# Two chains of attention layers: all seven product banks in one rotation, and a new table of ten value phases

## The chip, the cores and the metric

The kernel runs on one core of a Trainium2 chip. Five engines matter here: TensorE (PE in the profile; its weight loads are the row PEld), VectorE (DVE), ScalarE (ACT), GpSimd (POOL) and the queue of SyncE (SP) that issues the DMAs. The metric is the time of one execution on the device in microseconds; before the change it is 5680.44 us, the median of three runs (5678.14 to 5684.44).

## The reference, cut to what matters

Four residual layers run in the order A, B, A, B over one sequence of 2048 tokens with 576 features. In both kinds there are 32 heads of 18 features; in B all heads share one key and one value.

```python
S, D, H, Dh = 2048, 576, 32, 18
def _A_ref(x, wqkv, wo):
    q, k, v = (x @ wqkv) split into 3, H heads of Dh
    scores = einsum("bhqd,bhkd->bhqk", q, k) * (Dh ** -0.5)
    p = softmax(scores)
    return einsum("bhqk,bhkd->bhqd", p, v) @ wo        # heads joined again
def _B_ref(x, wq, wk, wv, wo):                          # the same, k and v without a head
...
x = x + _A_ref(_layernorm(x), A_wqkv, A_wo)
x = x + _B_ref(_layernorm(x), B_wq, B_wk, B_wv, B_wo)
x = x + _A_ref(_layernorm(x), A_wqkv, A_wo)
x = x + _B_ref(_layernorm(x), B_wq, B_wk, B_wv, B_wo)
```

Nearly all the work is the attention: per layer 32 heads of 2048 by 2048 scores, their exponentials, and the product with the values.

## The kernel before, in words

**Layers and units.** Each layer projects queries, keys and values (`project`, `natural`), attends, and projects the result back (`out_proj`). The attention goes by pairs of heads (`p`, 16 of them) and by quarters of 512 queries (`u`): 64 units a layer, 256 in all. A unit needs three kinds of product on TensorE:

- *scores* (`exp_mm`, L789 to L799): keys on the partitions, 512 queries along the free axis, 32 of them a unit (16 blocks of 128 keys for each head of the pair). The matmul is L795; ScalarE turns each bank into exponentials (L799, `pt<-pse`).
- *maxima* (`max_mm`, L556 to L589): the row maxima that the exponent subtracts have to be known first, so they come from a separate product with queries on the partitions and 512 keys along the free axis (L576), 32 a unit. VectorE reduces each bank to one column (L581, `mx<-psm`). Four times a unit two such products are *shared*: the product with the difference of two key blocks (L570) goes to ScalarE as a ReLU into the one SBUF tile `relu` (L574), and the product with the first of the two blocks is later joined with it on VectorE (L579, a custom instruction that adds and takes the maximum). So of 32 maximum products a unit ScalarE takes 4 and VectorE 28. `m_order` (L530 to L542) pairs each shared product with a partner: the first product of the same head that lies more than three products later and is not taken.
- *values* (`pv_block`, L812 to L829): exponentials times values into one bank, `oacc`, with 19 columns a head (18 features and a one that yields the sum). The 512 columns of one step of four exponentials can be cut anywhere, and `pv_cols` (L803) asks for so many columns at a time. After 8 steps, or 4096 columns, a unit is complete and ScalarE copies `oacc` out (L827, `oc<-oacc`).

The two heads of a pair lie on partitions 0 to 63 and 64 to 127, and a score or maximum product uses only its head's half of the array; two neighbouring products of different heads run side by side. Score and maximum products (512 columns wide) and value products use the array in different ways, so the kernel groups them.

**The order of the work.** It is written out by hand in `UNIT` (L65), a list of phases. Each phase is a row of products, such as `m0 e1 e0 m1 e0 m1` (`m` maximum, `e` score, the digit is the head), and a number of value columns to be done after it. Eleven phases make a unit: 32 scores, 32 maxima, 4096 columns. The maxima run ahead of the scores by `LEAD` = 14 steps of four, so those of a unit are complete shortly after the third phase of the unit before; `UNIT_X` (L73) lists which of the unit's 32 maxima are shared ones. The loop that walks the table is L925 to L936; the first two phases of a layer do no value columns. When the last maximum is done, a shorter loop (L940) finishes the scores.

**The banks.** One of the eight PSUM banks is `oacc`. Maxima take turns in three banks (`mtile`, L144) and scores in four (`etile`, L147). A product can't start before the reader of the bank's last product is done: for a score always ScalarE, for a maximum VectorE (ScalarE for a shared one). The projections outside the loop and the maxima that are woven into them use the same two functions.

**Small steps in the loop.** Once a unit `max_final` (L769) takes 128x32 to 128x8 on VectorE (L771, `neg<-mx`), GpSimd splits it, `max_store` (L777) transposes it on VectorE (L780, `tr<-hl`), and SyncE sends it through DRAM into two rows of the query tile (L782, L786). `o_sum`, `l_part`, `l_inv`, `l_out`, `l_rows`, `o_mul` and `o_out` normalise a finished unit on GpSimd with some DMAs. They stand in `todo` with due times counted in scores, and `run_todo` issues at the start of a phase what has come due.

Of the kernel before, what the change touches and what calls it, by code (L numbers as in the profile page):

```python
# [8 lines left out]
F32 = mybir.dt.float32  # L9
# [9 lines left out]
P = 128  # L19
NCH = S // P  # L20
NPAIR = H // 2
# [25 lines left out]
LEAD = 14  # L47
# [14 lines left out]

UNIT = [("m0 e1 e0 m1 e0 m1", 512), ("m0 e1 m1 e0 e1 m0", 416), ("e0 m1 m0 e1 e0 e1 m0", 416),  # L65
        ("m0 m1 e1 e0 m1", 192), ("e1 m0 m1 e0 e1 m0", 544), ("m1 e0 e0 m1 m0 e1", 352), ("e0 m1 e1 m0 m0 e1", 416),
        ("e0 m1 e0 e1 m1 m0 e1", 384), ("m0 m1", 32), ("e1 m0 e0 e1 e0 m1 m0", 448), ("e1 m0 m1 e0 e0 m1", 384)]
UNIT = [([(o[0], int(o[1])) for o in rows.split()], cols) for rows, cols in UNIT]

UNIT_X = (9, 17, 24, 30)  # L73


@with_exitstack
def tile_kernel(ctx: ExitStack, tc: tile.TileContext, A_x, A_wqkv, A_wo, B_x, B_wq, B_wk, B_wv, B_wo, out):
# [6 lines left out]
    psum = ctx.enter_context(tc.tile_pool(name="psum", bufs=1, space=PSUM))  # L84
# [56 lines left out]
        nc.gpsimd.memset(t, 0.0)  # L141


    def mtile(name):  # L144
        return psum.tile([P, 512], F32, tag="m", bufs=3, name=name)

    def etile(name):  # L147
        return psum.tile([P, 512], F32, tag="e", bufs=4, name=name)

    def ptile(name, shape=(P, 512), dt=F32):  # L150
        return pool.tile(list(shape), dt, tag="p", bufs=15, name=name)
# [208 lines left out]
    tail = []  # L360
# [31 lines left out]
    for layer in range(4):  # L392
# [125 lines left out]
        def ops(p):  # L518
            return big[:, q_slot(p)], big[:, k_slot(p)]


        m_next, m_done, m_count, m_full = [0, 0], [0], {}, []
# [6 lines left out]

        m_order, m_diff = [], set()  # L530
        for a in range(2):
            cycle = [g for rows, _ in UNIT for kind, g in rows if kind == "m"]
            n = -4 * LEAD % 32
            own = [(i, i % 32 in UNIT_X) for i in range(n, n + 32) if cycle[i % 32] == a]
            order = [None] * 16
            for qc, i in enumerate(i for i, x in enumerate(own) if x[1]):
                order[i] = qc, 1
                order[min(j for j, (at_, x) in enumerate(own) if at_ > own[i][0] + 3 and not x and not order[j])] = qc, 0
                m_diff.add((a, qc, 1))
            left = [(i // 2 % 4, i // 8 * 2 + i % 2) for i in range(16)]  # L540
            left = [x for x in left if x not in order]
            m_order.append([x or left.pop(0) for x in order])  # L542

        def max_place(a, i):

            p, u = divmod(i // 16, 4)
            if i < len(m_first):
                return (0, *m_first[i])
            n = i % 16
            return (p, u, *m_order[a][n]) if i >= 32 else (p, u, n // 2 % 4, n // 8 % 2 * 2 + n % 2)  # L550


        ns = STEPS * 4 * NPAIR
        m_heads = ([0, 1] * (2 * LEAD) + [g for rows, _ in UNIT for kind, g in rows if kind == "m"] * (4 * NPAIR))[:4 * ns]

        def max_mm(bank=mtile):  # L556

            i = m_done[0]
            a = m_heads[i]
            p, u, qc, kb = max_place(a, m_next[a])  # L560
            q, k = ops(p)
            if (p, u) not in mxs:
                mxs[p, u] = pool.tile([P, 32], F32, name="mx") if (p, u) < (0, 2) else mx2[u % 2]
            mx, ps = mxs[p, u], bank("psm")
            b, r = 64 * a, 16 * a + 4 * qc + kb
            c0 = u * 512 + qc * P
            if (p, u) >= (0, 2) and (a, qc, kb) in m_diff:
                assert kd_pair[p % 2 if is_a and p else 2] == (p if is_a else 0)
                k = kd(p)[b:b + 3 * DH]
                nc.tensor.matmul(ps.rearrange("p (h t) -> p h t", h=2) if p == 0 or not is_a else ps,  # L570
                                 q[b:b + 3 * DH, c0:c0 + P], k,
                                 start=True, stop=True)
                t = relus[p, u, a, qc] = relu[:, :512]
                nc.scalar.activation(t, ps, AF.Relu)  # L574
            else:
                nc.tensor.matmul(ps, q[b:b + KM, c0:c0 + P], k[b:b + KM, kb * 512:(kb + 1) * 512], start=True, stop=True)  # L576
                if kb == 0 and (p, u, a, qc) in relus:
                    t = relus.pop((p, u, a, qc))
                    nc.vector.tensor_tensor_reduce(t, ps, t, 1.0, LOWEST, OP.add, OP.max, mx[:, r:r + 1])  # L579
                else:  # L580
                    nc.vector.reduce_max(mx[:, r:r + 1], ps, axis=AX.X)  # L581
            m_next[a] += 1
            m_done[0] += 1
            while m_full and i >= m_full[0][1] + 2:
                max_final(*m_full.pop()[0])
            m_count[p, u] = m_count.get((p, u), 0) + 1
            if m_count[p, u] == 32:
                assert m_next[0] == m_next[1]
                m_full.append(((p, u), i))  # L589
# [3 lines left out]
        def kd(p):  # L593
            if p == 0 or not is_a:
                return big[:, 1::4, 7 * 256:]
            i = p % 2
            return xx_flat[:, 512 * i:512 * i + 512]
# [171 lines left out]
        def max_final(p, u):  # L769
            neg = pool.tile([P, 8], F32, name="neg")  # L770
            nc.vector.tensor_reduce(neg, mxs.pop((p, u)).rearrange("p (b k) -> p b k", k=4), axis=AX.X, op=OP.max,  # L771
                                    negate=True)
            hl = nms[p, u] = hls[(4 * p + u) % 2]
            copy(nc.gpsimd, hl[:, 0:8], neg)
            nc.gpsimd.tensor_tensor(hl[:, 8:16], neg, hl.bitcast(F32)[:, 0:8], op=OP.subtract)
# [10 lines left out]
                nc.sync.dma_start(big_f[64 * a + KM:64 * a + KE, q_slot(p), u * 512:(u + 1) * 512],  # L786
                                  m_d[u][:, a].rearrange("j q p -> j (q p)"))

        def exp_mm(p, u, i, tail):  # L789

            a, kc = (i // 2) % 2, i // 4 * 2 + i % 2
            q, k = ops(p)
            e = (mtile if tail and i % 2 else etile)("pse")
            r = 64 * a
            nc.tensor.matmul(e, k[r:r + KE, kc * P:(kc + 1) * P], q[r:r + KE, u * 512:(u + 1) * 512],  # L795
                             start=True, stop=True)

            pt = pts[p, u, i] = ptile("pt")
            nc.scalar.activation(pt, e, AF.Exp, scale=SCALE)  # L799
# [3 lines left out]
        def pv_cols(cols):  # L803

            while cols:
                n, c0 = divmod(pv_at[0], 512)
                w = min(cols, 512 - c0)
                pv_block(n, c0, c0 + w)
                pv_at[0] += w
                cols -= w  # L810

        def pv_block(n, c0, c1):  # L812

            p, u, i = *divmod(n // STEPS, 4), n % STEPS * 4
            cs = slice(c0, c1)
            turn[0] += 1
            for i in range(i, i + 4) if turn[0] % 2 else range(i + 3, i - 1, -1):
                a, kc = (i // 2) % 2, i // 4 * 2 + i % 2
                j = 64 * a + 32 * (kc % 2)
                nc.tensor.matmul(oacc[j:j + DH + 1, cs], v_of(kc)[:, 2 * p + a if is_a else 0, :], pts[p, u, i][:, cs],  # L820
                                 start=kc < 2 and c0 == 0, stop=kc >= 14 and c1 == 512)
                if c1 == 512:
                    pts.pop((p, u, i))
            if c1 == 512 and i // 4 == STEPS - 1:
                oc = ocs[p, u] = ptile("oc")
                if m_done[0] < 4 * ns:
                    nc.scalar.activation(oc, oacc, AF.Copy)  # L827
                else:
                    copy(nc.vector, oc, oacc)  # L829
# [43 lines left out]
        for p in range(NPAIR):  # L873
            for u in range(4):
                b = STEPS * (4 * p + u) + STEPS - 1
# [14 lines left out]
        for c in range(5):  # L890
# [3 lines left out]
            if layer < 3:  # L894
                b = LEAD + 32 * (NPAIR - 1) + 2 * c
# [6 lines left out]
        def run_todo(st):  # L902
            for n in sorted(n for n in todo if n <= st):
                for f, args in todo.pop(n):
                    f(*args)

        b = LEAD + ns
# [9 lines left out]
        assert not weave["left"] and m_done[0] == 4 * LEAD  # L917
        e_next = [0, 0]

        def exp_next(a):  # L920
            pu, kc = divmod(e_next[a], NCH)
            exp_mm(*divmod(pu, 4), kc // 2 * 4 + 2 * a + kc % 2, m_done[0] >= 4 * ns)
            e_next[a] += 1

        phase = 0  # L925
        while m_done[0] < 4 * ns:
            rows, cols = UNIT[phase % len(UNIT)]
            run_todo(LEAD + sum(e_next) / 4)
            for kind, a in rows:
                if kind == "e":  # L930
                    exp_next(a)
                elif m_done[0] < 4 * ns:
                    max_mm()
            if phase >= 2:
                pv_cols(cols)
            phase += 1  # L936
        while m_full:
            max_final(*m_full.pop()[0])
# [12 lines left out]
        tail = [todo.pop(n, []) for n in range(ns + LEAD + L_AT + 1, ns + LEAD + O_AT)]  # L951
# [32 lines left out]
```

## Time and profile before

| | |
|---|---|
| median of 3 runs | 5680.44 us (5678.14 to 5684.44) |
| profiled execution, span | 5684.0 us (3.6 us above the median; the profile gives no other time for it) |
| PE busy | 5650.3 us, 99% |
| PEld busy | 3010.8 us, 53% |
| DVE busy | 4917.2 us, 87% |
| ACT busy | 4932.6 us, 87% |
| POOL busy | 1836.8 us, 32% |
| from the start of one unit's scores to the next, inside the loop | 18.9 us |

The span has four stages that look alike, one a layer: some 200 us of projections, in which VectorE and ScalarE are partly idle, then close to 1200 us of the loop. A busy time is the time in which at least one instruction of the engine was running; instructions of one engine overlap in the records, so a busy share near 100% doesn't say that nothing more would fit in. In the rows of the timeline the columns are the start, the length, the engine, the line and operation, and how many instructions of that kind the row joins; brackets tell for how long the engine was idle before it and which work released it.

### The profile page before, as it was taken

To read this page: it belongs to the slowest core of one execution; us is meant where nothing else is said; L and a number is where in the kernel's file an instruction comes from. 1 tells how busy PE (TensorE), PEld (TensorE's weight loads), DVE (VectorE), ACT (ScalarE), POOL (GpSimd) and SP (SyncE) were. 2 spreads that over 40 slices of the span, in tenths; PEclk is the share of its full clock that TensorE was granted. 3 is DMA by queue.
4 is the path that set the end of the run, shared out by engine and by line. 5 is a ranking of instruction groups with operands and counts; after the bars stand their busy time and mean duration, and the time that the engine had idled before them with its cause. 6 is when DMAs were issued, how large, how long until landed. Compare 5 with 4: busy or idle time off the path is not lost.

```text
span 5684.0 us, 148130 instructions
## 1 busy us (share of the span) xinstructions
PE 5650.3 (99%) x57758; PEld 3010.8 (53%) x57758; DVE 4917.2 (87%) x9489; ACT 4932.6 (87%) x9872; POOL 1836.8 (32%) x2396
## 2 busy tenths in 40 slices
PE   9999999999999999999999999999999999999999
PEld 8644444444844444444686444444448444444446
DVE  4799999997699999999637999999976999999995
ACT  2599999999289999999726999999992999999996
POOL 3243333334233333233312433333332332323232
PEclk9999999999999999999999999999999999999999
DMA  6321111111420000001253211111114100000002
GB/s 206 120 58 42 44 44 45 42 44 26 128 68 23 23 21 23 20 23 24 60 172 105 54 47 41 46 42 46 39 34 130 56 23 23 23 24 20 23 15 79
DMA packets 275207, 301.97 MB, mean 53 GB/s; under 512 B 135247, under 2 KB 193191, under 8 KB 265215
## 3 DMA queue, kind: packets, MB, share of 16 engines
q1 hardware_dynamic: 274502, 292.49, 18.4%
q8 instruction: 453, 7.42, 0.5%
q14 instruction: 252, 2.06, 0.1%
HBM read 168.50 MB, written 119.86 MB: 51 GB/s over the span
## 4 chain that ended last, share of the span: by engine, by line
PE 95%; POOL 1%; DMA 1%; issue 1%; DVE 1%; SPq 0%; ACT 0%; POOLq 0%; DVEq 0%; ACTq 0%
PE oacc L820 37%; PE pse L795 23%; PE psm L576 18%; PE psn L240 6%; PE psm L570 5%; PE psq L414 5%; DVE mx L581 1%; PE ps L232 0%; POOL big L186 0%; DMA raw<-in_B_wk_dram 0%; DMA m_d<-tr 0%; DMA big<-qk_d 0%; DMA big<-m_d 0%; DMA qk_d<-ev 0%; POOL ev L426 0%
## 5 line engine op out<-in xcount | busy, mean ns | idle before, releaser
L799 ACT ACTIVATE pt<-pse 128x512 f32<-128x512 f32 x8192 | 4262.6, 642 | 98.8 <-PE pse L795 61.8
L581 DVE TENSOR_REDUCE mx<-psm 128x1 f32<-128x512 f32 x6208 | 3931.1, 685 | 313.0 <-PE psm L576 132.7
L576 PE MATMUL psm<-big 62*128 62x512 f32 x7200 | 2665.8, 452 | 7.1 <-DMA big<-qk_d 4.0
L795 PE MATMUL pse<-big 64*128 64x512 f32 x8192 | 2411.4, 429 | 5.6 <-ACT pt L799 3.3
L820 PE MATMUL oacc<-pt,vbuf 128*19 128x96 f32 (+3 forms) x27536 | 1754.9, 361 | 3.5 <-DVE oc L157 3.5
L795 PEld LDWEIGHTS pse<-big 64*128 64x128 f32 x8192 | 1191.8, 185 | 784.5 <-ACT pt L799 602.3
L576 PEld LDWEIGHTS psm<-big 62*128 62x128 f32 x7200 | 1164.1, 184 | 381.4 <-DVE mx L581 231.6
L820 PEld LDWEIGHTS oacc<-pt,vbuf 128*19 128x19 f32 x27536 | 530.2, 98 | 782.2 <-issue 652.0
L157 POOL TENSOR_SCALAR os<-oc 32x512 f32<-32x512 f32 x512 | 314.5, 614 | 1923.1 <-ACT oc L827 1532.3
L846 POOL TENSOR_TENSOR rl<-lt,mone 128x8 f32<-128x8 f32 x256 | 423.2, 1653 | 1099.4 <-DMA lt<-os 1045.4
L579 DVE CUSTOM_DVE_ANT_0 relu<-psm,relu 128x512 f32<-128x512 f32 x992 | 676.7, 682 | 0.0
L574 ACT ACTIVATE relu<-psm 128x512 f32<-128x512 f32 x992 | 616.2, 621 | 1.5 <-PE psm L570 0.8
L820 PE MATMUL oacc<-pt,vy 128*19 128x256 f32 (+3 forms) x9168 | 591.4, 360 | 0.0
L422 ACT ACTIVATE ev<-psq 128x512 fp32r<-128x512 f32 (+1 forms) x112 | 67.1, 599 | 335.0 <-PE psq L414 233.3
L820 PEld LDWEIGHTS oacc<-pt,vy 128*19 128x19 f32 x9168 | 206.0, 98 | 267.9 <-issue 220.0
L859 POOL TENSOR_TENSOR os<-os,rb 96x512 f32<-96x512 f32 x256 | 327.8, 1280 | 27.4 <-DMA rb<-r_d 26.3
L837 POOL TENSOR_TENSOR os<-os,oc 96x512 f32<-96x512 f32 x256 | 327.0, 1277 | 21.4
L240 PE MATMUL psn<-wsm,xx 128*128 128x288 f32 x2240 | 308.0, 296 | 0.0
L240 PEld LDWEIGHTS psn<-wsm,xx 128*128 128x128 f32 x2240 | 298.7, 188 | 12.9 <-issue 11.6
L428 DVE TENSOR_TENSOR ev<-psq,ev 128x512 fp32r<-128x512 f32 (+1 forms) x84 | 58.0, 691 | 213.5 <-ACT ev L422 199.6
L570 PE MATMUL psm<-big 54*128 54x512 f32 x512 | 240.7, 470 | 0.0
L570 PE MATMUL psm<-xx,big 54*128 54x512 f32 x480 | 225.0, 469 | 0.0
(93 smaller groups left out, 2378.8 us busy)
## 6 DMA issues: line engine op xcount, KB each, us to landing
big<-qk_d SPq DMA_DIRECT2D x172, 432.0 KB
qk_d<-ev SPq DMA_DIRECT2D x96, 512.0 KB
qk_d<-ev SPq DMA_DIRECT2D x120, 256.0 KB
rb<-r_d SPq DMA_DIRECT2D x512, 36.0 KB
o_d<-os SPq DMA_DIRECT2D x512, 36.0 KB
m_d<-tr SPq DMA_DIRECT2D x1024, 2.0 KB
o<-o_d SPq DMA_DIRECT2D x64, 256.0 KB
xx<-qk_d SPq DMA_DIRECT2D x120, 72.0 KB
```

Of the source, the lines that this page charges most:

```text
L240: nc.tensor.matmul(ps, lhs[:, xc, :], wsm[:, wc, h * 288:(h + 1) * 288], start=i == 0, stop=i == len(TERMS) - 1)
L570: nc.tensor.matmul(ps.rearrange("p (h t) -> p h t", h=2) if p == 0 or not is_a else ps, q[b:b + 3 * DH, c0:c0 + P], k, start=True, stop=True)
L574: nc.scalar.activation(t, ps, AF.Relu)
L576: nc.tensor.matmul(ps, q[b:b + KM, c0:c0 + P], k[b:b + KM, kb * 512:(kb + 1) * 512], start=True, stop=True)
L579: nc.vector.tensor_tensor_reduce(t, ps, t, 1.0, LOWEST, OP.add, OP.max, mx[:, r:r + 1])
L581: nc.vector.reduce_max(mx[:, r:r + 1], ps, axis=AX.X)
L795: nc.tensor.matmul(e, k[r:r + KE, kc * P:(kc + 1) * P], q[r:r + KE, u * 512:(u + 1) * 512], start=True, stop=True)
L799: nc.scalar.activation(pt, e, AF.Exp, scale=SCALE)
L820: nc.tensor.matmul(oacc[j:j + DH + 1, cs], v_of(kc)[:, 2 * p + a if is_a else 0, :], pts[p, u, i][:, cs], start=kc < 2 and c0 == 0, stop=k ...
L837: nc.gpsimd.tensor_tensor(t[:96], t[:96], oc[:96], op=OP.add)
L846: nc.gpsimd.tensor_tensor(rl, lts.pop((p, u)), mone, op=OP.pow)
L859: nc.gpsimd.tensor_tensor(t[:96], t[:96], rb[:96], op=OP.mult)
```

## The change

All seven banks go into one list ordered by last use. In the loop a product no longer takes the next bank of its own kind: it takes the bank longest unused (rank 0) or the second longest unused (rank 1), whoever reads it, and the third character in the table gives the rank. Outside the loop `mtile` and `etile` still take turns over three and four banks. The table has ten phases instead of eleven, all with six or seven products, and the kind `r` marks a shared maximum in the table itself: three a unit in place of four, all of head 1, at the places 14, 16 and 26 among the unit's 32 maxima (counted from 0). `m_order` gives them the partners 18, 21 and 31. The 928 value columns that the first two phases of a layer skipped are now counted out by `PV_LAG`; the first two phases of the new table have 928 columns as well.

```diff
-UNIT = [("m0 e1 e0 m1 e0 m1", 512), ("m0 e1 m1 e0 e1 m0", 416), ("e0 m1 m0 e1 e0 e1 m0", 416),
-        ("m0 m1 e1 e0 m1", 192), ("e1 m0 m1 e0 e1 m0", 544), ("m1 e0 e0 m1 m0 e1", 352), ("e0 m1 e1 m0 m0 e1", 416),
-        ("e0 m1 e0 e1 m1 m0 e1", 384), ("m0 m1", 32), ("e1 m0 e0 e1 e0 m1 m0", 448), ("e1 m0 m1 e0 e0 m1", 384)]
-UNIT = [([(o[0], int(o[1])) for o in rows.split()], cols) for rows, cols in UNIT]
-UNIT_X = (9, 17, 24, 30)
+UNIT = [("e01 m10 e00 m10 m00 e11", 384),
+        ("m10 e00 m10 e00 e10 m01", 544),
+        ("e10 m01 e10 m01 m10 e00", 384),
+        ("e10 m00 e10 e00 m10 e01", 352),
+        ("m10 m00 e10 m00 e01 r10", 416),
+        ("m00 e10 r11 e00 m11 e00 m10", 416),
+        ("m01 e10 e10 e11 m00 e01 m10", 384),
+        ("m10 e00 m00 e11 m00 e11", 384),
+        ("m00 r10 e00 m01 e10 m01 e10", 416),
+        ("m11 e00 e00 m00 e10 e00 m10", 416)]
+UNIT = [([(o[0], int(o[1]), int(o[2])) for o in rows.split()], cols) for rows, cols in UNIT]
+PV_LAG = 928
+UNIT_M = [(kind, a) for rows, _ in UNIT for kind, a, _ in rows if kind != "e"]
...
+    lru, turns = list(range(7)), {"m": 0, "e": 0}
+    def bank(i, name):
+        lru.remove(i)
+        lru.append(i)
+        return psum.tile([P, 512], F32, tag=f"b{i}", bufs=1, name=name)
     def mtile(name):
-        return psum.tile([P, 512], F32, tag="m", bufs=3, name=name)
+        turns["m"] += 1
+        return bank((turns["m"] - 1) % 3, name)
     def etile(name):
-        return psum.tile([P, 512], F32, tag="e", bufs=4, name=name)
+        turns["e"] += 1
+        return bank(3 + (turns["e"] - 1) % 4, name)
+    def oldest(rank=0):
+        return lambda name: bank(lru[rank], name)
...
-            own = [(i, i % 32 in UNIT_X) for i in range(n, n + 32) if cycle[i % 32] == a]
+            own = [(i, UNIT_M[i % 32][0] == "r") for i in range(n, n + 32) if UNIT_M[i % 32][1] == a]
...
-        def exp_mm(p, u, i, tail):
+        def exp_mm(p, u, i, rank):
-            e = (mtile if tail and i % 2 else etile)("pse")
+            e = oldest(rank)("pse")
...
             rows, cols = UNIT[phase % len(UNIT)]
             run_todo(LEAD + sum(e_next) / 4)
-            for kind, a in rows:
+            for kind, a, rank in rows:
                 if kind == "e":
-                    exp_next(a)
+                    exp_next(a, rank)
                 elif m_done[0] < 4 * ns:
-                    max_mm()
-            if phase >= 2:
-                pv_cols(cols)
+                    max_mm(oldest(rank))
+            skip = min(cols, PV_LAG - lagged)
+            lagged += skip
+            pv_cols(cols - skip)
             phase += 1
```

More of the change, by code (lines that the diff above doesn't have):

```diff
@@ L60 @@
 TAIL = 2
-UNIT = [("m0 e1 e0 m1 e0 m1", 512), ("m0 e1 m1 e0 e1 m0", 416), ("e0 m1 m0 e1 e0 e1 m0", 416),
-        ("m0 m1 e1 e0 m1", 192), ("e1 m0 m1 e0 e1 m0", 544), ("m1 e0 e0 m1 m0 e1", 352), ("e0 m1 e1 m0 m0 e1", 416),
-        ("e0 m1 e0 e1 m1 m0 e1", 384), ("m0 m1", 32), ("e1 m0 e0 e1 e0 m1 m0", 448), ("e1 m0 m1 e0 e0 m1", 384)]
-UNIT = [([(o[0], int(o[1])) for o in rows.split()], cols) for rows, cols in UNIT]
-UNIT_X = (9, 17, 24, 30)
+UNIT = [("e01 m10 e00 m10 m00 e11", 384),
[11 more added lines that the diff above has]
+UNIT_M = [(kind, a) for rows, _ in UNIT for kind, a, _ in rows if kind != "e"]
+assert len(UNIT_M) == 32 and sum(cols for _, cols in UNIT) == 4096
 @with_exitstack
@@ L531, in tile_kernel @@
         for a in range(2):
-            cycle = [g for rows, _ in UNIT for kind, g in rows if kind == "m"]
             n = -4 * LEAD % 32
-            own = [(i, i % 32 in UNIT_X) for i in range(n, n + 32) if cycle[i % 32] == a]
+            own = [(i, UNIT_M[i % 32][0] == "r") for i in range(n, n + 32) if UNIT_M[i % 32][1] == a]
             order = [None] * 16
@@ L553, in tile_kernel @@
         ns = STEPS * 4 * NPAIR
-        m_heads = ([0, 1] * (2 * LEAD) + [g for rows, _ in UNIT for kind, g in rows if kind == "m"] * (4 * NPAIR))[:4 * ns]
+        m_heads = ([0, 1] * (2 * LEAD) + [a for _, a in UNIT_M] * (4 * NPAIR))[:4 * ns]
         def max_mm(bank=mtile):
@@ L918, in tile_kernel, with exp_next @@
         e_next = [0, 0]
-        def exp_next(a):
+        def exp_next(a, rank=0):
             pu, kc = divmod(e_next[a], NCH)
-            exp_mm(*divmod(pu, 4), kc // 2 * 4 + 2 * a + kc % 2, m_done[0] >= 4 * ns)
+            exp_mm(*divmod(pu, 4), kc // 2 * 4 + 2 * a + kc % 2, rank)
             e_next[a] += 1
-        phase = 0
+        phase = lagged = 0
         while m_done[0] < 4 * ns:
```

## The prediction, made before the changed kernel was run

> **What bounds the kernel now.** I read the page first, for the engines and the costliest groups:
>
> ```profile
> PE 5650.3 (99%) x57758; PEld 3010.8 (53%) x57758; DVE 4917.2 (87%) x9489; ACT 4932.6 (87%) x9872; POOL 1836.8 (32%) x2396
> ...
> L799 ACT ACTIVATE pt<-pse 128x512 f32<-128x512 f32 x8192 | 4262.6, 642 | 98.8 <-PE pse L795 61.8
> L581 DVE TENSOR_REDUCE mx<-psm 128x1 f32<-128x512 f32 x6208 | 3931.1, 685 | 313.0 <-PE psm L576 132.7
> ```
>
> Then the stage that fills most of the time, the loop of the first layer, by its busy times and by the waits of TensorE's weight loads:
>
> ```profile
> 420.00:1180.00 760.00, 760.00 (x8379) 364.16 (x8375) 714.08 (x1369) 746.51 (x1490) 264.95 (x331) 1.00 0.17 44
> ```
>
> ```profile
> PEld pse L795 <- ACT pt L799: 95.8, 188, 0.7
> PEld psm L570 <- DVE mx L581: 44.9, 81, 0.7
> ```
>
> Three engines look full: TensorE 760 of 760 us, ScalarE 746.5, VectorE 714.1. Busy times don't settle which one sets the pace, since records overlap. So I went to the timeline of one unit and read starts instead of lengths. I number the phases of a table from 0; a "stretch" is the score and maximum products of a phase, a "value part" the columns behind it. TensorE, with the start of each first row (phases 1, 2, 4, 5, 8, 9, and phase 1 of the next unit):
>
> ```profile
> 804.70 0.50 PE L576 MATMUL psm<-big 62*128 62x512 f32 x1
> ...
> 805.73 0.90 PE L820 MATMUL oacc<-pt,vy 128*19 128x416 f32 x8
> 806.56 0.50 PE L795 MATMUL pse<-big 64*128 64x512 f32 x1
> ...
> 807.68 0.90 PE L820 MATMUL oacc<-pt,vbuf 128*19 128x416 f32 x8
> ...
> 809.95 0.50 PE L795 MATMUL pse<-big 64*128 64x512 f32 x1
> ...
> 810.86 1.11 PE L820 MATMUL oacc<-pt,vbuf 128*19 128x416 f32 x16
> 811.90 0.49 PE L576 MATMUL psm<-big 62*128 62x512 f32 x1
> ...
> 817.35 0.50 PE L576 MATMUL psm<-big 62*128 62x512 f32 x1
> 817.78 0.25 PE L820 MATMUL oacc<-pt,vy 128*19 128x32 f32 x8
> 817.97 0.50 PE L795 MATMUL pse<-big 64*128 64x512 f32 x1
> ...
> 823.60 0.50 PE L576 MATMUL psm<-big 62*128 62x512 f32 x1
> ```
>
> A unit takes 823.60 - 804.70 = 18.90 us. Value parts take 0.19 us for 32 columns (817.78 to 817.97), 0.83 for 416 (805.73 to 806.56) and 1.04 for 544 (810.86 to 811.90): 0.13 us plus 1.667 ns a column, however they are cut. Stretches take 0.43 us for one pair of products (817.35 to 817.78), 0.91 for three (809.95 to 810.86), 1.12 to 1.13 for four (806.56 to 807.68): 0.20 us plus 0.234 a pair. Phase 1 has three pairs, yet takes 1.03: a wait of 0.12.
>
> Without waits, the old table costs TensorE 11 x (0.20 + 0.13) + 34 pairs x 0.234 + 4096 x 1.667 ns = 3.63 + 7.96 + 6.83 = 18.42 us. (I counted the pairs from the table: a seven-product stretch takes four, a five-product one three.) So waits cost 18.90 - 18.42 = 0.48 us a unit. What one looks like, in phase 5:
>
> ```profile
> 811.73 0.68 DVE L579 CUSTOM_DVE_ANT_0 relu<-psm,relu 128x512 f32<-128x512 f32 x1
> ...
> 811.91 0.50 PE L795 MATMUL pse<-big 64*128 64x512 f32 x1
> ...
> 812.24 0.39 PE L576 MATMUL psm<-big 62*128 62x512 f32 x1
> ...
> 812.33 0.21 DVE L780 STREAM_TRANSPOSE tr<-hl 128x32 f32<-128x32 f32 x1
> 812.46 1.26 DVE L581 TENSOR_REDUCE mx<-psm 128x1 f32<-128x512 f32 x2
> 812.47 1.09 ACT L799 ACTIVATE pt<-pse 128x512 f32<-128x512 f32 x2 [0.16 <-PE pse L795]
> 812.47 0.18 PEld L570 LDWEIGHTS psm<-xx,big 54*128 54x128 f32 x1 [0.27 <-DVE mx L579]
> ...
> 812.90 0.14 PEld L820 LDWEIGHTS oacc<-pt,vbuf 128*19 128x19 f32 x8 [0.25 <-issue]
> ```
>
> The custom reduce ends at 812.41; the weights of the third pair load at 812.47, 0.57 after the stretch began. The value part follows 0.43 later, at 1.00 in place of 0.91, so a load at 0.47 would have cost nothing. From these rows, four constants. Pairs start at 0, 0.34, 0.57 and 0.81; their weights must load by 0, 0.23, 0.47 and 0.70. A first pair's product can be read 0.56 after its start (811.91 to 812.47); later pairs' records are 0.1 shorter (0.39 against 0.50), so at 0.80, 1.03, 1.27. A bank is free 0.06 after its reader's end.
>
> The readers' own pace is start to start. VectorE and ScalarE:
>
> ```profile
> 808.93 0.18 DVE L771 TENSOR_REDUCE neg<-mx 128x8 f32<-128x32 f32 x1
> 809.08 1.29 DVE L581 TENSOR_REDUCE mx<-psm 128x1 f32<-128x512 f32 x2
> ...
> 814.20 3.08 DVE L581 TENSOR_REDUCE mx<-psm 128x1 f32<-128x512 f32 x5 [0.48 <-PE pse L795]
> 817.20 0.68 DVE L579 CUSTOM_DVE_ANT_0 relu<-psm,relu 128x512 f32<-128x512 f32 x1
> ...
> 817.92 1.93 DVE L581 TENSOR_REDUCE mx<-psm 128x1 f32<-128x512 f32 x3
> ```
>
> ```profile
> 806.78 0.62 ACT L827 ACTIVATE oc<-oacc 128x512 f32<-128x512 f32 x1
> 807.26 2.11 ACT L799 ACTIVATE pt<-pse 128x512 f32<-128x512 f32 x4
> 809.17 0.69 ACT L574 ACTIVATE relu<-psm 128x512 f32<-128x512 f32 x1
> 809.65 2.66 ACT L799 ACTIVATE pt<-pse 128x512 f32<-128x512 f32 x5
> ```
>
> Five reduces from 814.20 to 817.20 give 0.60 each; the custom one takes 0.72 to the next reduce, the small reduce 0.15, the transpose 0.13. VectorE needs 24 x 0.60 + 4 x 0.72 + 0.28 = 17.6 of 18.9 us. Every ScalarE instruction takes 0.48 start to start, though it lasts 0.64: 37 x 0.48 = 17.8. **TensorE sets the pace**, 18.42 plus waits for banks.
>
> **The change part by part.**
>
> *One phase less.* The new table has ten phases; I count 34 pairs and 4096 columns again. TensorE without waits: 10 x 0.33 + 7.96 + 6.83 = 18.09 us, 0.33 less. Value parts are cut at 17 places instead of 18, which the rows price at nothing. The skipped columns stay 928. Nothing hides this term, because TensorE is the path.
>
> *One ReLU less, one reduce more.* ScalarE: 36 x 0.48 = 17.3 us. VectorE: 26 x 0.60 + 3 x 0.72 + 0.28 = 18.04 of 18.09. VectorE, with 1.3 us to spare a unit before, has 0.05. It can't run without a gap (the products come in bursts), so TensorE will go on waiting for it. Off the path, GpSimd and the DMAs keep their work; the transpose stays at the start of phase 5, the max rows' DMAs at phase 8.
>
> *The shared banks.* A bank returns after six to eight products of any kind instead of three maxima or four scores. I walked one unit of the new table with the constants above, each product taking the bank that ranks give it. Four places cost time:
> - Phase 3, last product (e01): its bank held the last score of phase 2. The copy of `oacc` starts 0.22 into phase 2 (806.78 against 806.56), so the phase's three exponentials start at 0.70, 1.18, 1.66, and the third lasts 0.61 (1.09 less 0.48, from the pair at 812.47) and frees its bank at 1.66 + 0.61 + 0.06 = 2.33. Phase 3 begins after 0.91 + 0.77 = 1.68 and must load by 1.68 + 0.47 = 2.15. Wait 0.18.
> - Phase 5, second score of head 0 (e00, in the third pair): its bank held the third maximum of phase 4, where VectorE, idle before, starts at 0.57, 1.16, 1.76; free at 2.50. Deadline 1.73 + 0.47 = 2.20. But phase 5 has seven products and head 0 has no product in the fourth pair, so 0.23 of the 0.30 are absorbed. Cost 0.07. The old table shows this: its seven-product stretches end on time.
> - Phase 7, last product (e11): bank of the custom reduce that ends phase 6. From phase 4 VectorE runs without a gap: 0.57 + 7 x 0.60 + 0.72 + 0.13 = 5.61 to its start, 6.35 to free. Phases 4 to 6 take 1.73 + 2.03 + 1.90 = 5.66, deadline 6.13. Wait 0.22.
> - Phase 0, last product (e11): bank of the custom reduce of phase 9, which starts at 0.57 + 2 x 0.60 = 1.77 and frees at 2.51. Deadline 1.96 + 0.47 = 2.43. Wait 0.08.
>
> That is 0.55 us. The same walk through the old table gives 0.41, where the rows show 0.48. So I take 0.61, between 0.55 and 0.55 x 0.48 / 0.41 = 0.64. Its own bounds are one wait such as phase 3's less or more, rounded to 0.46 and 0.76, as VectorE has no slack for another burst.
>
> *One tile for two ReLUs.* The shared products at places 14 and 16 write the same `relu` tile before partner 18 reads it, so the partner's reduce waits for the second ReLU. By the walk that ReLU ends 3.44 us after phase 4 begins and VectorE comes to the partner at 3.68: no wait, with 0.24 to spare.
>
> *The sum.* A unit takes 18.09 + 0.61 = 18.70 us, 0.20 less than 18.90. Each layer's loop begins with 56 of 2048 maxima done, which leaves 62 units; four layers make 248. 248 x 0.20 = 50 us. Against its own span: 5684.0 - 50 = 5634; the median of the runs lies 3.6 us lower, so 5680.4 - 50 = **5631 us**. Lead, tail and projections keep their order of work and are costed at nothing.
>
> **The skill's rule.** Row first: in the loop ScalarE is busy for 746.5 of 760 us, 98%, TensorE's weight loads for 364.2, 48%. The Trainium skill, "Perfetto Trace Analysis", section "Identifying the Most-Contended Engine", says to judge ScalarE and VectorE by occupancy, TensorE by MFU and the busy share of weight loads, and to call the engine with the highest share the bottleneck. By that rule ScalarE would be the bound, and the time would fall by the ReLU alone. This trace speaks against it: a 0.64 us exponential is followed by the next after 0.48.
>
> **The rivals.**
> - *ScalarE is the bound* (the rule's case). Then a ReLU of 0.48 less a unit gives 248 x 0.48 = 119 us: 5561. For it: 98% busy and the largest wait of TensorE (95.8 us in 188 waits). Against: starts leave 1.1 us a unit free. Freer banks that cut the waits from 0.48 to 0.33 would land there too. Chance 0.14.
> - *No change.* The waits take the whole phase: 0.81 instead of 0.48. VectorE at 18.04 of 18.09 speaks for it, the walk against it. 5680. Chance 0.13.
> - *Slower: the second ReLU is late.* If ScalarE reaches it 0.60 us later than walked, VectorE stalls 0.60 - 0.24 = 0.36, the bank at phase 7 comes so much later, and 0.36 - 0.20 = 0.16 a unit makes 40 us: 5720. It decides from 0.44 us late. For it: waits in phases 3 to 5 delay exponentials ahead of it. Against: ScalarE has 1.4 us a unit free. Chance 0.13.
>
> The forecast keeps 0.60.
>
> **How the numbers follow.** The forecast's own span, waits 0.46 to 0.76, is 18.55 to 18.85 us a unit: 248 x (0.35 to 0.05) is 87 to 12 us, 5593 to 5668. To hold eight in ten I go a little into each neighbour: 5580 to 5675. A measurement of this kernel tells some 0.2%, 11 us, from nothing. Faster: 0.59 of the forecast and the first rival's 0.14, 0.73. Within: 0.01 and most of the second, 0.12. Slower: the third and the rest, 0.15.
>
> **What would show it.** Right: 18.6 to 18.8 us from unit to unit, ten value parts; ScalarE idle longer, VectorE 97% by starts; late weight loads at the ends of phases 3 and 7, behind `pt` and the custom reduce; the ReLU of place 16 done before its partner's reduce. Wrong: 18.4 or less (waits gone, or ScalarE was the bound), or VectorE idle ahead of the custom reduce with a ReLU as its releaser.

## The result and the profile after

The changed kernel takes 5591.98 us (median, 5589.68 to 5593.45), the one before in the same runs 5682.44 us. The ratio is 0.9837, with a 95% interval from 0.9823 to 0.9851: 90 us faster. The prediction had 50 us, 5631, and a range of 5580 to 5675 that holds the result.

The page of the changed kernel, the engines and the costliest groups of ScalarE and VectorE (busy us, mean ns of one, idle time before them):

```profile
PE 5549.8 (99%) x55774; PEld 3117.2 (56%) x55774; DVE 4999.5 (89%) x9489; ACT 4843.4 (87%) x9624; POOL 1835.7 (33%) x2396
...
L598 DVE TENSOR_REDUCE mx<-psm 128x1 f32<-128x512 f32 x6704 | 4181.8, 682 | 148.4 <-PE psm L593 90.8
L816 ACT ACTIVATE pt<-pse 128x512 f32<-128x512 f32 x8192 | 4195.7, 614 | 55.2 <-PE pse L812 9.6
```

The same stretch of the loop as before, its busy times and the waits of TensorE's weight loads:

```profile
420.00:1180.00 760.00, 760.00 (x8223) 389.49 (x8221) 741.48 (x1397) 747.33 (x1480) 268.77 (x338) 1.00 0.18 45
```

```profile
PEld pse L812 <- DVE mx L598: 69.6, 123, 0.8
PEld psm L593 <- ACT pt L816: 58.9, 124, 0.6
PEld psm L593 <- DVE mx L598: 26.1, 41, 0.6
```

VectorE went from 714 to 741 busy us of 760 and its reduces' idle time in the whole run from 313.0 to 148.4 us. Scores now wait for VectorE, and maxima more for ScalarE than for VectorE; before, each waited for its own reader. These are idle times of the weight loads, and much of them lies under value parts, so they are no sum of what TensorE lost.

That sum comes from the pace. ScalarE copies the value bank once a unit. Its row in the window, before and after (count, lengths in ns, first and last start in us):

```profile
L827 ACT ACTIVATE oc<-oacc x40: 618/621/623, 429.0 to 1165.6; 128x512 f32<-128x512 f32 x40
```

```profile
L844 ACT ACTIVATE oc<-oacc x41: 597/598/600, 426.9 to 1166.9; 128x512 f32<-128x512 f32 x41
```

Before, 736.6 us for 39 units, 18.89 each; after, 740.0 for 40, **18.50**. The forecast was 18.70.

### The profile page after: what moved, and what is told of

Same layout as the page of the kernel before. It is cut to its first block, busy times and chain, and to the rows that moved or that the text cites. A ratio compares the mean times of both kernels' runs of the same rounds, so it can differ in the third digit from the quotient of the medians.

```text
span 5591.6 us, 144494 instructions
## 1 busy us (share of the span) xinstructions
PE 5549.8 (99%) x55774; PEld 3117.2 (56%) x55774; DVE 4999.5 (89%) x9489; ACT 4843.4 (87%) x9624; POOL 1835.7 (33%) x2396
## 4 chain that ended last, share of the span: by engine, by line
PE 95%; POOL 2%; DMA 1%; issue 1%; SPq 1%; DVE 0%; ACT 0%; POOLq 0%; ACTq 0%; DVEq 0%
PE oacc L837 37%; PE psm L593 24%; PE pse L812 21%; PE psn L258 7%; PE psq L432 5%; PE psm L587 1%; PE ps L250 0%; DMA big<-qk_d 0%; POOL big L204 0%; POOL ev L444 0%; DMA raw<-in_B_wq_dram 0%; DMA raw<-in_B_wk_dram 0%; DVE mx L598 0%; DMA big<-m_d 0%; DMA xo<-in_A_x_dram 0%
## 5 line engine op out<-in xcount | busy, mean ns | idle before, releaser
L598 DVE TENSOR_REDUCE mx<-psm 128x1 f32<-128x512 f32 x6704 | 4181.8, 682 | 148.4 <-PE psm L593 90.8
L816 ACT ACTIVATE pt<-pse 128x512 f32<-128x512 f32 x8192 | 4195.7, 614 | 55.2 <-PE pse L812 9.6
L593 PE MATMUL psm<-big 62*128 62x512 f32 x7448 | 2563.9, 440 | 11.6 <-ACT pt L816 8.8
L812 PE MATMUL pse<-big 64*128 64x512 f32 x8192 | 2557.6, 437 | 7.9 <-DMA big<-m_d 5.6
L837 PE MATMUL oacc<-pt,vbuf 128*19 128x384 f32 (+8 forms) x26544 | 1735.9, 368 | 4.3 <-DVE oc L175 3.9
L175 POOL TENSOR_SCALAR os<-oc 32x512 f32<-32x512 f32 x512 | 313.0, 611 | 1791.8 <-ACT oc L844 1538.6
L837 PE MATMUL oacc<-pt,vy 128*19 128x288 f32 (+3 forms) x8176 | 570.9, 383 | 0.0
L596 DVE CUSTOM_DVE_ANT_0 relu<-psm,relu 128x512 f32<-128x512 f32 x744 | 507.0, 681 | 0.9 <-ACT relu L591 0.9
L591 ACT ACTIVATE relu<-psm 128x512 f32<-128x512 f32 x744 | 445.7, 599 | 38.3 <-PE psm L587 18.5
L432 PE MATMUL psq<-yx,big 128*128 128x512 f32 (+2 forms) x826 | 195.9, 389 | 3.5 <-ACT evr L443 1.8
L432 PE MATMUL psq<-xx,big 128*128 128x512 f32 (+1 forms) x784 | 195.0, 399 | 1.8 <-ACT evr L443 1.8
```

The source lines that it names most:

```text
L432: nc.tensor.matmul(ps[:n].rearrange("p (u t) -> p u t", u=2)[:, us], w[:, wc, :n], xts[T][:, us, xc, :], start=(xc, wc) == TERMS[0], stop= ...
```

## The experiments

Eleven kernels, each beside the kernel before, with the new kernel at 5592 us for comparison. "The walk" is the one of the prediction, with its constants. Pace of a unit is taken from the row of the value bank's copy, as above.

**The banks as before under the new table.**

```diff
-            e = oldest(rank)("pse")
+            e = etile("pse")
...
-                    max_mm(oldest(rank))
+                    max_mm()
```

> The new table with its ten phases and three shared maxima, but the banks as before: maxima take turns in three, scores in four. Theory (TensorE's path is its starts plus the waits for banks, and the new rows need the common rotation): phase 4 puts four of its six products on the three maximum banks, and three stretches hold four, so a bank asked for again within its stretch is not free for over a microsecond; walked with the starts and ends of the trace of before, a unit comes to some 20.7 us, 2.2 more than now, 248 units: about 6130 us. Rival (the gain is the phase that fell away, and who shares banks with whom hardly matters): 5590 to 5620 us.

Measured: **6125.56 us** (ratio to before 1.0779, 1.0763 to 1.0795). The pace:

```profile
L844 ACT ACTIVATE oc<-oacc x37: 597/598/602, 426.6 to 1172.1; 128x512 f32<-128x512 f32 x37
```

745.5 us for 36 units, 20.71. The three stretches with four maximum products take 1.71 us instead of 0.90 and 1.13 to 1.17. These rows can't be had without the common rotation; a ten-phase table arranged for banks of three and four wasn't tried.

**The common rotation under the old table.**

```diff
-UNIT = [("e01 m10 e00 m10 m00 e11", 384), ...
+UNIT = [("m00 e10 e00 m10 e00 m10", 512), ...     # the eleven old phases, rank 0 everywhere
```

> The old table of eleven phases with its four shared maxima, but with the seven banks in one rotation, the longest unused first (rank 0 everywhere). Rival (the common rotation by itself gives the gain, since a bank returns after seven products): the waits of 0.48 us a unit shrink, 5600 to 5640 us. Theory (a bank's place in the order says nothing of when its reader ends; a table must be fitted to it): maxima wait behind late exponentials and scores behind late reduces, the walk gives 0.8 us a unit more than before, 248 units: about 5880 us.

Measured: 5875.88 us (1.0341, 1.0325 to 1.0356), a pace of 19.71. The rotation alone loses 194 us. As tried, neither half of the change is worth anything without the other. The old table with ranks fitted to it wasn't tried, so the runs don't say how much of the gain needs the new rows.

**A phase more.**

```diff
-        ("m10 e00 m10 e00 e10 m01", 544),
+        ("m10 e00", 32),
+        ("m10 e00 e10 m01", 512),
```

> The new kernel with phase 1 cut in two: its first two products with 32 value columns, then the other four with 512. Pairs, columns, banks and shares stay. Theory (each phase costs TensorE 0.33 us of switching that nothing hides): 0.33 x 248 = 81 us more than the new kernel, about 5673 us; if the extra stop lets readers catch up, some of the 0.41 us of waits goes and it is less, not under 5640. Rival (VectorE sets the pace, 18.0 of 18.5 us a unit): a stop of TensorE costs little, 5592 to 5610 us.

Measured: 5652.8 us, 61 more than the new kernel, a pace of 18.77:

```profile
L845 ACT ACTIVATE oc<-oacc x40: 598/599/601, 429.8 to 1162.0; 128x512 f32<-128x512 f32 x40
```

The one phase took 0.93 + 1.04 us, the two take 0.43 + 0.19 + 0.67 + 0.99 (means over the loop of the first layer): 0.30 more. Of the forecast 0.33 the rest is the 0.03 that phase 1 had waited. Readers catch up little elsewhere. A phase more gives ScalarE and VectorE no work, and yet 61 of the 90 us are lost again. So most of what the change gained, 0.39 us a unit, is the phase that fell away.

**Ranks set to 0.**

```diff
-UNIT = [("e01 m10 e00 m10 m00 e11", 384), ...
+UNIT = [("e00 m10 e00 m10 m00 e10", 384), ...     # the same rows, rank 0 everywhere
```

> The new kernel with rank 0 in every place: always the bank longest unused, never the second longest. Rows, columns, shares and phases stay. Theory (what counts is when a bank's reader ends; the rank picks between two banks the one that is free first): three places now ask for a bank whose reader is late, in phases 0, 1, 3 and 5, and the walk gives 0.8 us a unit more than the new kernel, 248 units: about 5790 us. Rival (an order by last use is good enough, ranks are a detail): 5592 to 5610 us.

Measured: 5810.29 us (1.0222, 1.0207 to 1.0237), a pace of 19.43, against 5790 expected. Rows and shares are those of the fast kernel; the seventeen ranks of 1 are worth 218 us in this table. Phases 0, 1, 3 and 5 take 0.10 to 0.23 us longer, as expected, and so does phase 7 (0.20), which wasn't named.

**One ReLU more, one less.**

```diff
-        ("m10 e00 m00 e11 m00 e11", 384),
+        ("m10 e00 r00 e11 m00 e11", 384),
```

```diff
-        ("m00 r10 e00 m01 e10 m01 e10", 416),
+        ("m00 m10 e00 m01 e10 m01 e10", 416),
```

> The new kernel with a fourth shared maximum a unit: the second maximum of phase 7 becomes one, so ScalarE has a ReLU more (0.48 us a unit) and VectorE a reduce less (0.60). Theory (TensorE's starts plus the waits that the table leaves): the waits at phases 3, 5, 7 and 0 stay where they are, since they are made ahead of that place, and one product of phase 8 waits 0.14 us longer for a bank that the ReLU now holds: 0.14 x 248 = 34 us more, about 5625 us. Rival one (ScalarE sets the pace): 119 us more, about 5710. Rival two (VectorE, at 18.0 of 18.5 us, sets the pace): up to 0.4 us a unit less, 5500 to 5560 us.

> The new kernel with two shared maxima a unit: the one of phase 8 becomes a plain maximum. ScalarE has 35 starts of 0.48 = 16.8 us, VectorE 28 x 0.60 + 2 x 0.70 + 0.25 = 18.5. Theory (VectorE's work in the second half of the unit makes the waits): the reduce stands in the busiest stretch of VectorE, the last products of phase 9 wait for the banks, 0.4 us a unit more, 248 units: about 5695 us. Rival (ScalarE sets the pace, so the change gained by its one ReLU less): another 119 us less, about 5475 us.

Measured: 5643.6 and 5683.73 us, 52 and 92 more than the new kernel; 34 and 103 were expected. Paces of 18.73 and 18.90. Both directions lose. If ScalarE set the pace, the ReLU more would have cost 119 us, and it cost 52; if VectorE did, that run would have gained. The ReLU less decides nothing between the two: it gives VectorE a reduce more, 18.5 us a unit by its own count, so a kernel bound by ScalarE needn't have gained either. With a ReLU more, one stretch of seven products, phase 8, grows from 1.13 to 1.39 us. Weight loads and ScalarE there, from the timeline of that run:

```profile
816.70 0.18 PEld L593 LDWEIGHTS psm<-big 62*128 62x128 f32 x1 [0.48 <-ACT relu L591]
...
817.67 0.18 PEld L593 LDWEIGHTS psm<-big 62*128 62x128 f32 x1 [0.30 <-ACT pt L816]
```

```profile
816.00 0.64 ACT L591 ACTIVATE relu<-psm 128x512 f32<-128x512 f32 x1
816.47 1.14 ACT L816 ACTIVATE pt<-pse 128x512 f32<-128x512 f32 x2
```

The bank that the new ReLU holds (816.00 to 816.64) comes back as the stretch begins. The late one is held by the second exponential behind it, which ends at 817.61: the fourth pair loads at 817.67, 0.97 into the stretch and 0.27 after its deadline of 0.70. With a ReLU less, the last stretch grows from 1.15 to 1.55. What counts is which bank is late where.

**Half of each plain reduce.**

```diff
-                    nc.vector.reduce_max(mx[:, r:r + 1], ps, axis=AX.X)
+                    nc.vector.reduce_max(mx[:, r:r + 1], ps[:, :256] if (p, u) >= (0, 2) else ps, axis=AX.X)
```

> The new kernel, but the plain reduces take the maximum over 256 of the 512 columns of their bank: half of those keys are left out of the row maxima. TensorE, ScalarE, the table and the ranks stay; VectorE needs about 11 us a unit instead of 18. Theory (waits at phases 5, 7 and 0 are for VectorE, the one at phase 3 for ScalarE): only 0.17 us at phase 3 remains, a unit of 18.27 us, 0.23 less than now, 57 us: about 5535 us. Rival one (ScalarE sets the pace): no change, 5585 to 5600. Rival two (TensorE's own time is not 18.1 us but less, and VectorE holds it back throughout): under 5500 us.

Measured: 5552.65 us, 39 less than the new kernel; 57 were expected. VectorE's busy time and the pace:

```profile
420.00:1180.00 760.00, 760.00 (x8274) 377.92 (x8274) 497.93 (x1406) 751.70 (x1491) 270.95 (x340) 1.00 0.17 45
```

```profile
L844 ACT ACTIVATE oc<-oacc x42: 597/598/600, 423.8 to 1176.7; 128x512 f32<-128x512 f32 x42
```

752.9 us for 41 units, 18.36. With VectorE down from 741 to 498 busy us, phase 3 still takes 1.06 us instead of 0.90, as in the new kernel, while phases 5 and 7 lose their waits. Phase 0 loses its 0.03 too; phases 1 and 9 keep small waits, 0.06 and 0.02. So phase 3 waits for ScalarE, phases 0, 5 and 7 waited for VectorE, and TensorE's own time, 18.36 less the 0.17 at phase 3 and some 0.1 of small waits, is the 18.1 of the prediction.

**Other tables.** Four tables were fitted by the walk.

```diff
+# four shared maxima:  ("r12 m02 m01 e10 e10 e01 m10", 416), ("m12 e00 m00 e11 e10 m01", 512), ...
+# refitted:            ("r02 m11 e10 m00 m02 e10", 384), ("e00 m11 m10 e00 e10 m00 e10", 448), ...
+# refitted b:          ("e00 m11 m00 e00 e11 e00 m10", 448), ("m02 e11 m01 m10 e00 e11", 480), ...
+# refitted c:          ("e01 m10 e10 m01 e00 e10 m00", 448), ("e00 m11 e12 m01 e02 m10", 480), ...
```

> Another table of ten phases and 34 pairs, fitted by the walk, with four shared maxima a unit instead of three and ranks up to 2, one rotation of seven banks (and the last piece of value columns kept from going below zero). ScalarE has 37 starts of 0.48 = 17.8 us, VectorE 24 x 0.60 + 4 x 0.70 + 0.25 = 17.5. Theory (TensorE's starts of 18.1 plus waits; waits come from VectorE being full): VectorE has 0.5 us a unit more room, waits fall to 0.1 to 0.2, a unit of 18.2 to 18.3 us, 50 to 75 us less than the new kernel: 5515 to 5545 us. Rival (ScalarE sets the pace): one ReLU more is 0.48 x 248 = 119 us more, about 5710 us. Second rival (the gain came from the fourth ReLU's going): 5640 us or more.

> Another table fitted by the walk, after correcting it by the run with four shared maxima (the second pair of a stretch starts 0.34 us after the first even where the first was late; the walk had it at 0.23): ten phases, 34 pairs, three shared maxima a unit whose partners follow before the next one, ranks 0 to 2. TensorE's own time and the readers' work are those of the new kernel; only the order differs. Theory (the new table's 0.41 us of waits are a matter of order): the walk leaves 0.15 us, 0.27 us a unit less, 248 units: 5525 to 5540 us. Rival (VectorE needs 18.0 of 18.1 us, so no order can bring the unit much below 18.5): 5580 us or more.

> A table fitted by the walk like the last one, but with the 4096th value column of a unit at the end of a phase, so that ScalarE's copy of the value bank has a stretch of products to hide behind; the last table had it inside a phase, where the next columns stood and waited for the copy, 1.6 us a unit. Ten phases, 34 pairs, three shared maxima whose partners follow before the next one. Theory (the 0.41 us of waits are a matter of order): the walk gives 0.25 us a unit less than the new kernel, 248 units: about 5530 us. Rival (VectorE needs 18.0 us a unit and any order leaves its gaps): 5580 us or more.

> A second table fitted in the same way and with the same conditions, in which the walk leaves more of the late banks in stretches of seven products, where a late product finds a free half-slot. Theory: 0.26 us a unit less than the new kernel by the walk, about 5528 us, if the free half-slots take up the lateness as the old table's did; if they don't, the late products cost up to 0.4 us more and it comes to 5620 us. Rival (no order gets below VectorE's own pace): 5580 us or more.

Measured: 5675.58, 5984.55, 5600.85 and 5583.57 us. Three missed what the walk expected of them; the fourth lies between its two values. All four lie where a rival had them, the first at 5640 or more and the others at 5580 or more.

The first table has six stretches of seven products, so 35 pairs and not the 34 that its expectation counts: TensorE's own time is 18.32 us by the prediction's constants, above the 18.2 to 18.3 expected for the whole unit. Its pace is 18.68, so waits are 0.36 us, where 0.1 to 0.2 were walked: the walk had started the second pair of a stretch 0.23 us after a late first one, where the trace has 0.34, and the fitting had made use of that. The pace makes 45 of the 84 us that this run is above the new kernel; the rest lies outside the steady loop and wasn't followed up. The rival (the gain came from the fourth ReLU's going) isn't needed for it, as the waits are no larger than the new kernel's 0.41. In the second, a unit's 4096th column lies inside a phase, and the value part stands still for the copy:

```profile
465.99 0.62 ACT L844 ACTIVATE oc<-oacc 128x512 f32<-128x512 f32 x1
...
466.66 0.89 PE L837 MATMUL oacc<-pt,vbuf 128*19 128x416 f32 x8 [1.37 <-ACT oc L844]
```

The value part, 512 columns, takes 2.56 us there instead of the 0.98 that 0.13 us and 1.667 ns a column make. The third and fourth, at paces of 18.52 and 18.46 us, came 0.22 to 0.27 us a unit above the walk. The fourth, ratio 0.9827 (0.9812 to 0.9841), can't be told from the new kernel's 0.9837 (0.9823 to 0.9851). No table tried is clearly better than the new one, and whether any order of these products goes clearly below 18.4 us a unit stays open: the rival that VectorE allows none is neither shown nor excluded.

## Why the prediction was right in direction and half the size

**The number.** The phase was priced rightly, and the wait term had the wrong sign: from the old table's 0.48 us a unit to 0.61 by the forecast, to 0.41 by the runs (18.50 less 18.09). So the unit gained 0.33 and some 0.07 more, where the forecast took 0.13 off. The pace of 18.50 lies between the 18.6 to 18.8 that the prediction called right and the 18.4 that it called wrong, and 5592 us lies 1 us below the 5593 to 5668 of the forecast's own span. The range holds it only because it was stretched a little towards the first rival, and that rival's reason, ScalarE as the bound, isn't what the runs show.

**TensorE sets the pace, and a phase costs 0.33 us.** Right. The eleventh phase put back 0.30 of it, and with VectorE relieved the pace falls towards 18.1 us and not below.

**ScalarE as the bound.** ScalarE was busy for 98% of the loop before and still is (747.3 of 760 us) in a kernel that is 1.6% faster; so the sign "ScalarE idle longer" didn't show in its busy time. Giving it a ReLU more cost 52 us, where ScalarE as the bound asks for 119, and a phase more cost 61 without any work for it. Records of 0.61 us that start every 0.48 fill a row without filling the engine. The runs so decide against the rule of the Trainium skill, "Perfetto Trace Analysis", section "Identifying the Most-Contended Engine", that the prediction set beside this rival: there the engine with the highest occupancy is the most contended one.

**The shared banks: the places were right, the sizes weren't.** The step that failed is "So I take 0.61": measured are 0.40. Waits of TensorE by place (mean over the loop of the first layer: length of the stretch less 0.90 for three pairs, 1.13 for four):

| phase | walked | measured |
|---|---|---|
| 0, last product | 0.08 | 0.03 |
| 1 | 0 | 0.03 |
| 3, last product | 0.18 | 0.17 |
| 5, e00 | 0.07 | 0.04 |
| 7, last product | 0.22 | 0.11 |
| 9 | 0 | 0.02 |
| sum | 0.55, taken as 0.61 | 0.40 |

Two errors make the difference of 0.21. Scaling 0.55 up by the old table's shortfall added 0.06, and what the old walk had missed was no constant share of the waits. And the walk took VectorE too slow. VectorE from phase 4 to phase 6 of the new kernel:

```profile
819.19 1.89 DVE L598 TENSOR_REDUCE mx<-psm 128x1 f32<-128x512 f32 x3 [0.21 <-PE psm L593]
820.99 0.20 DVE L797 STREAM_TRANSPOSE tr<-hl 128x32 f32<-128x32 f32 x1
821.12 1.25 DVE L598 TENSOR_REDUCE mx<-psm 128x1 f32<-128x512 f32 x2
822.28 0.68 DVE L596 CUSTOM_DVE_ANT_0 relu<-psm,relu 128x512 f32<-128x512 f32 x1
...
822.92 1.29 DVE L598 TENSOR_REDUCE mx<-psm 128x1 f32<-128x512 f32 x2
824.13 0.68 DVE L596 CUSTOM_DVE_ANT_0 relu<-psm,relu 128x512 f32<-128x512 f32 x1
```

It runs without a gap, as walked. But the custom reduce costs 0.64 us to the next start (822.28 to 822.92), where the prediction took 0.72 from a place where VectorE had waited a little (the pair of 817.35 can be read 0.56 later, at 817.91, and the next reduce starts at 817.92). From 819.19 to 824.13 are 4.94 us, the prediction had 5.05. Phase 4 begins at 818.65, so the first reduce starts after 0.54, not 0.57. What that does to phase 7:

```profile
824.29 0.18 PEld L593 LDWEIGHTS psm<-big 62*128 62x128 f32 x1 [0.64 <-DVE mx L598]
...
824.87 0.18 PEld L812 LDWEIGHTS pse<-big 64*128 64x128 f32 x1
825.30 0.14 PEld L837 LDWEIGHTS oacc<-pt,vbuf 128*19 128x19 f32 x8 [0.24 <-issue]
```

The last product's weights load at 824.87, 0.06 after the custom reduce ends at 824.81, and 0.58 into the stretch: 0.11 after the deadline of 0.47. The mechanism is the one that was walked, at half the price. At phase 0 it is the same: the custom reduce of phase 9 starts 1.74 into its phase instead of 1.77 and costs less, and phase 9 with its value part takes 1.98 instead of 1.96. Phase 3 shows the other mechanism, behind the copy of `oacc`:

```profile
833.92 0.60 ACT L844 ACTIVATE oc<-oacc 128x512 f32<-128x512 f32 x1
834.41 3.57 ACT L816 ACTIVATE pt<-pse 128x512 f32<-128x512 f32 x7
```

```profile
835.38 0.18 PEld L812 LDWEIGHTS pse<-big 64*128 64x128 f32 x1 [0.64 <-DVE mx L598]
...
836.04 0.18 PEld L812 LDWEIGHTS pse<-big 64*128 64x128 f32 x1
...
836.47 0.23 PEld L837 LDWEIGHTS oacc<-pt,vbuf 128*19 128x19 f32 x10 [0.24 <-issue]
```

The third exponential behind the copy starts at 835.37 and ends at 835.99. The load comes 0.05 later, at 836.04, 0.66 into the stretch and 0.19 late, and the value part at 1.09 instead of 0.90.

**The second ReLU.** No stall: before 744 custom reduces VectorE was idle for a ReLU for 0.9 us in all. But a wait was the smaller question. By the code, the second ReLU overwrites the first before its partner reads it, and the partner's custom instruction writes its own sum into the same tile, which the second partner then takes for its ReLU. The two ReLUs of the unit above both run before its first custom reduce at 822.28, and no ReLU comes between that one and the next at 824.13:

```profile
820.40 0.61 ACT L591 ACTIVATE relu<-psm 128x512 f32<-128x512 f32 x1
820.96 0.60 ACT L816 ACTIVATE pt<-pse 128x512 f32<-128x512 f32 x1
821.45 0.59 ACT L591 ACTIVATE relu<-psm 128x512 f32<-128x512 f32 x1
821.93 4.56 ACT L816 ACTIVATE pt<-pse 128x512 f32<-128x512 f32 x9
```

So in two blocks of 128 queries a unit the number subtracted from the exponents is not the row's maximum. It falls out in the division by the sum, as long as no exponential overflows. The kernel before doesn't do this, nor do the four fitted tables, and the last of them, at 5583.57 us, is no slower, so the time gained doesn't hang on it.

**The sum.** 248 x 0.39 is 97 us; the two profiled spans differ by 92.4. The loops of the four layers, 62 units each, took 4698.3 us before and 4614.0 after, 84 less: the starts of the loops and a few units near their ends gained nothing or became slower, by up to 1.9 us. All else together took 8 us less. That last part wasn't tried by itself.

## What to carry to other kernels

When two engines empty the same banks, give each product the bank whose reader ends first, and fit the order of the products to that: the rotation alone lost 194 us, the ranks were worth 218. Read the pace of an engine from starts, not from busy time, and price a switch between two uses of the array by lines through several widths. A walk with measured constants found the places of the larger waits, but tables fitted to it use up its errors, so the next fit has to be measured before it is believed.

## What the runs showed of the hardware that wasn't expected

Units of the new kernel take 18.45 and 18.55 us in turn. The copy of the value bank starts 0.16 us into its stretch in one and 0.22 in the next, the exponentials behind it shift by the same 0.06, and phase 3 takes 1.03 or 1.09 us. The value products of a unit come in 17 pieces, as a phase's columns are cut where a step ends, and the kernel turns round the order of the four products in every piece; an odd count makes successive units differ. That the order is the cause was only argued from this.

A product that is late in a stretch of seven can cost less than its lateness. The weight loads of phase 7 of the kernel before, which begins at 815.36:

```profile
815.36 0.18 PEld L795 LDWEIGHTS pse<-big 64*128 64x128 f32 x1 [0.64 <-ACT pt L799]
...
816.14 0.18 PEld L576 LDWEIGHTS psm<-big 62*128 62x128 f32 x1 [0.24 <-DVE mx L581]
...
816.57 0.14 PEld L820 LDWEIGHTS oacc<-pt,vbuf 128*19 128x19 f32 x8 [0.25 <-issue]
```

A maximum of the third pair loads 0.78 into the stretch, 0.31 after its deadline of 0.47, and the value part still follows at 1.21 instead of 1.13. Only 0.08 is lost, as if that half of the array had used the fourth pair's free slot of 0.23. So the prediction's "its seven-product stretches end on time" holds for phases 2 and 9 of the old table (1.13 us each) and not quite for phase 7.
